# The second model's weights group by group instead of pair by pair, in a fused attention and expert kernel

## Chip, cores and metric

The kernel runs on one core of a Trainium2 chip. The metric is device time in microseconds, the median of three runs. The host only lays the inputs out; all arithmetic is on the core.

## The reference, cut to what matters

```python
kv = einsum('bhsd,bhse->bhde', k, v);  o = einsum('bhsd,bhde->bhse', q, kv)
x = (o / rms(o) * g_norm) as (2304, 512)
h = x @ w_in;  x = (h * sigmoid(h)) @ w_out          # first model, 2048 hidden units
p = domain_probs / (domain_probs.sum(-1) + 1e-9)
for e in range(4):                                   # second model, 1024 hidden units each
    out += p[:, e:e+1] * (maximum(x @ w1[e], 0) @ w2[e])
```

## The kernel before

The 2304 tokens are worked in three **pairs** of 768 tokens, each two halves of 384. The hidden units are cut into **groups** of 512: four groups of the first model, eight of the second (two for each expert). One **step** is one group for one pair: a first product (512 features to 512 hidden units), the activation, and a second product (512 hidden units to 512 outputs) that is added to `acc` in SBUF. Steps -12 to -1 belong to the first model, 0 to 23 to the second.

Every float32 operand of a product is split into a high part (rounded, by ScalarE, `hi`) and a low part (the rest, by VectorE or GpSimd, `lo`), and a product of blocks takes three matmul terms. A block product (`product`, L382 to 390) is 12 matmuls of 384 columns. A first product is always done with seven block products instead of eight (`first`, table `A`, `B`, `INTO`): that wants sums of weight blocks (`sumw`: s1 to s4) and sums of feature blocks (`xsum`: t1 to t4). A second product is done either plainly (`second`, eight block products, tile `ps_o`, 96 matmuls) or with seven (`again`, tiles `ps_ox` and `ps_oz`, 84 matmuls), which wants four sums of hidden blocks (`sumh`), three more hidden splits, and seven additions to `acc` (`gather`) instead of four. `seven(n)` says which steps use seven: before, steps 8 to 23, and five steps of the first model.

The order of the work is written out as events with slots (`events`, `seven_events`, `first_events`): a list of (slot, function), sorted, and emitted once. One slot is one block product on TensorE. `start[n]` is the slot at which step n begins; in a stretch of 14 or 15 slots TensorE alternates the seven first products of step n (slots 1, 3, 5, ...) with the second products of step n-1 (slots 0, 2, 4, ...). Each engine takes its instructions in that order, and so does SyncE's DMA queue (SP).

In the second model the **pair is the outer loop** (`pair(n) = n // 8`). The three pairs would each need all weights, so steps 0 to 7 make the split weights of a group (four loads of raw weights for each of the two matrices, eight sums, fourteen splits) and `put_away` writes them to `w_dram`; steps 8 to 23 `get` fourteen tiles of 512 KB each from there. The split features of a pair stay in SBUF for eight steps (`x_p`, seven tiles), and are made anew at steps 0, 8 and 16. Steps 0 to 7 have plain second products. When a pair is done, `leave` transposes it (L556), in later steps, and ScalarE's queue writes it out; the last pair leaves through `leave_last`.

```python
def seven(self, n): return n >= E2 or n in (-8, -7, -5, -4, -3)
def pair(self, n):  return (n + F1) % NP if n < 0 else n // E2
self.start[n + 1] = self.start[n] + (self.LONG if n <= E2 else self.SHORT)   # 15 or 14
```

Of the kernel before, what the change touches and what calls it, by code (L numbers as in the profile page):

```python
# [8 lines left out]
F32 = mybir.dt.float32  # L9
# [11 lines left out]
DM = H * D  # L21
# [44 lines left out]
class Net:  # L66
# [6 lines left out]

    A = ("a11", "a12", "s2", "s1", "s3", "s4", "a22")
# [9 lines left out]
    LONG, SHORT = 15, 14  # L84
    LEAD = 8

    def __init__(self, tc, dram, const, w, wd, out):
# [3 lines left out]
        self.p_dram, self.w_dram, self.x_dram = dram  # L91
# [8 lines left out]
        self.x, self.w1, self.wf, self.w2, self.raw, self.s, self.h, self.f, self.t, self.ps, self.pb = (  # L100
            {} for _ in range(11)
        )
# [26 lines left out]
    def plain_again(self):  # L129
        self.stacks["seven"].close()  # L130
        self.pb_p = self.open("left", "pb", 2)
        self.o_p = self.open("left", "o2", 2)
        self.s3_p = self.open("left", "s3", 3)
        self.raw3_p = self.open("left", "raw3", 4)

    def swap(self):
        self.stacks["conv"].close()
        self.s_p = self.open("sums", "s", 3, side="right")
        self.raw_p = self.open("sums", "raw", 8, side="right")

    def change(self):
        self.stacks["sums"].close()
        self.t_p = self.open("right", "t", 5, side="right")
        self.h7_p = self.open("right", "hid7", 1, side="right")

    def close(self):
        for k in ("right", "left", "psum"):
# [11 lines left out]

    def key(self, n):  # L160
        return n if n < 0 else n // E2
# [122 lines left out]
    def load1(self, n, i, j):  # L284
        t = self.raw_p.tile([128, 2, 2, 128], F32, tag="raw", name="raw1")
        for c in range(2):
            src = self.w[4 * n + 2 * i + c, :, 0, 256 * j : 256 * j + 256]
            self.nc.sync.dma_start(out=t[:, c, :, :].rearrange("p k f -> p (k f)"), in_=src)
        self.raw[n, 1, f"a{i + 1}{j + 1}"] = t.rearrange("p c k f -> p (c k f)")

    def load2(self, n, i, j, sums=False):
        pool = self.raw3_p if sums else self.raw_p
        t = pool.tile([128, 2, 256], F32, tag=pool.name, name=pool.name)
        for c in range(2):
            self.nc.sync.dma_start(out=t[:, c, :], in_=self.w[4 * n + 2 * j + c, :, 1, 256 * i : 256 * i + 256])
        self.raw[n, 2 + sums, f"a{i + 1}{j + 1}"] = t.rearrange("p c f -> p (c f)")

    def load_p(self, t, e):
        b = self.pb_p.tile([128, PW], F32, tag="pb", name="pb")
        src = self.p_dram.rearrange("(e b) k -> e (b k)", e=4)[e, t * PW : t * PW + PW]  # L300
        self.nc.sync.dma_start(out=b, in_=src.partition_broadcast(128))
        self.pb[t, e] = b

    def sumw(self, n, i, name, eng=None):
        a, b, op = self.SUMS[name]
        pool = self.s_p if i == 1 else self.s3_p
        t = pool.tile([128, 512], F32, tag=pool.name, name=pool.name)
        (eng or self.nc.vector).tensor_tensor(t, self.raw[n, i, a], self.raw[n, i, b], op=op)  # L308
        self.raw[n, i, name] = t

    def op1(self, n, k, eng=None):
        t = self.w1_p.tile([128, 2, 512], F32R, tag="w1", name="w1")
        self.split(t, self.raw[n, 1, self.A[k]], eng)
        self.w1[n, k] = t

    def op2(self, n, name, eng=None):
        pool, tag = (self.w2_p, "w2") if name[0] == "a" else (self.w1_p, "w1")
        t = pool.tile([128, 2, 512], F32R, tag=tag, name="w2")
# [759 lines left out]
```

## Time and profile before

| | before |
|---|---|
| median of 3 runs (lowest to highest) | 1168.19 us (1168.1 to 1168.59) |
| the profiled execution's own time | 1168.03 us |
| its span, first to last instruction | 1166.2 us |
| granted TensorE clock | 1.00 of full speed |
| TensorE (PE) busy | 1153.6 us, 99% |
| VectorE (DVE) busy | 866.8 us, 74% |
| ScalarE (ACT), GpSimd (POOL) busy | 499.1 us, 315.5 us |
| moved by DMA | 309 MB, mean 265 GB/s |

The profile is of one execution. Its parts used below: the page's head; the groups of instructions by line (busy time, mean ns of one, and the idle time of the engine ahead of them); the timeline, which gives start and duration of merged instructions and, in brackets, how long the engine had been idle before and who released it; the windows, which give busy time by engine in a stretch; and the DMA issues. PE's matmuls overlap, so a matmul's duration there is not the pitch at which they follow.

### The profile page before, as it was taken

How to read it: one execution, taken by the hardware profiler on the slowest of the kernel's cores; microseconds unless marked ns; L12 is line 12 of the kernel's file. 1: busy time of each engine (PE TensorE's matmuls, PEld its weight loads, DVE VectorE, ACT ScalarE, POOL GpSimd, SP SyncE). 2: the span in 40 equal slices, each digit the busy share in tenths (PEclk: the TensorE clock that was granted, in tenths of full speed). 3: DMA queues.
4: the chain of work that ended last, by engine and by line, in shares of the span. 5: the costliest groups of instructions: out<-in, count | busy, mean ns of one | idle time of the engine just before them, and what ended most of it. 6: DMA issues, size and time to landing. Idle time of an engine off the chain costs nothing.

```text
span 1166.2 us, 17617 instructions
## 1 busy us (share of the span) xinstructions
PE 1153.6 (99%) x6769; PEld 1144.8 (98%) x6769; DVE 866.8 (74%) x1010; ACT 499.1 (43%) x720; POOL 315.5 (27%) x196
## 2 busy tenths in 40 slices
PE   9999999999999999999999999999999999999998
PEld 8999999999999999999999999999999999999997
DVE  3997566887887667777777866777888866666776
ACT  4895565455544445434344324333233333233222
POOL 4943311232221324222232312121114221111112
PEclk9999999999999999999999999999999999999999
DMA  9876877566556366987896869898988777878764
GB/s 369 345 270 228 331 256 261 200 212 245 198 189 227 137 203 227 325 296 279 303 324 260 287 222 360 319 330 312 332 312 285 244 258 255 275 258 283 252 199 126
DMA packets 101815, 309.00 MB, mean 265 GB/s; under 512 B 11420, under 2 KB 37988, under 8 KB 101220
## 3 DMA queue, kind: packets, MB, share of 16 engines
q1 hardware_dynamic: 99716, 304.69, 73.6%
q10 hardware_dynamic: 2016, 3.18, 0.7%
q8 instruction: 54, 0.88, 0.3%
q14 instruction: 29, 0.24, 0.1%
HBM read 227.84 MB, written 79.99 MB: 264 GB/s over the span
## 4 chain that ended last, share of the span: by engine, by line
PE 54%; DVE 6%; ACT 2%; issue 2%; DMA 0%; SPq 0%; DVEq 0%; ACTq 0%
PE ps_x L390 15%; PE ps_z L390 11%; PE ps_o L526 10%; PE ps_ox L390 10%; PE ps_oz L390 8%; DVE f L469 1%; ACT hid L164 1%; DVE acc L495 1%; DVE f L433 1%; DVE hid L167 1%; DVE t L477 1%; DVE w L167 1%; PE ps_t L556 0%; DVE s L308 0%; ACT x L164 0%
## 5 line engine op out<-in xcount | busy, mean ns | idle before, releaser
L390 PE MATMUL ps_x<-x,w 128*128 128x384 f32 x1584 | 297.0, 335 | 0.0
L390 PEld LDWEIGHTS ps_x<-x,w 128*128 128x128 f32 x1584 | 277.6, 188 | 0.0
L526 PE MATMUL ps_o<-hid,w 128*128 128x384 f32 x1440 | 268.3, 335 | 1.5 <-ACT hid L164 1.4
L526 PEld LDWEIGHTS ps_o<-hid,w 128*128 128x128 f32 x1440 | 251.2, 188 | 3.4 <-ACT hid L164 2.4
L164 ACT ACTIVATE hid<-f 128x768 fp32r<-128x768 f32 x143 | 120.1, 843 | 243.3 <-DVE f L469 217.5
L390 PE MATMUL ps_z<-x,w 128*128 128x384 f32 x1188 | 222.9, 335 | 0.6 <-DVE f L433 0.6
L390 PEld LDWEIGHTS ps_z<-x,w 128*128 128x128 f32 x1188 | 208.2, 188 | 0.9 <-DVE f L433 0.9
L390 PE MATMUL ps_ox<-hid,w 128*128 128x384 f32 x1008 | 190.2, 336 | 1.2 <-DVE acc L495 1.0
L390 PEld LDWEIGHTS ps_ox<-hid,w 128*128 128x128 f32 x1008 | 176.2, 188 | 2.1 <-ACT hid L164 0.9
L167 DVE TENSOR_TENSOR hid<-f,hid 128x768 fp32r<-128x768 f32 x116 | 124.3, 1072 | 60.6 <-ACT hid L164 59.4
L390 PE MATMUL ps_oz<-hid,w 128*128 128x384 f32 x756 | 142.1, 335 | 1.6 <-DVE acc L495 1.2
L390 PEld LDWEIGHTS ps_oz<-hid,w 128*128 128x128 f32 x756 | 131.9, 188 | 2.7 <-DVE acc L495 2.1
L167 POOL TENSOR_TENSOR hid<-t,hid 128x768 fp32r<-128x768 f32 x32 | 62.7, 1961 | 241.8 <-ACT hid L164 236.0
L167 POOL TENSOR_TENSOR hid<-f,hid 128x768 fp32r<-128x768 f32 x27 | 52.3, 1938 | 210.7 <-ACT hid L164 210.7
L167 POOL TENSOR_TENSOR w<-raw,w 128x512 fp32r<-128x512 f32 x41 | 60.9, 1491 | 178.3 <-ACT w L164 135.2
L164 ACT ACTIVATE hid<-t 128x768 fp32r<-128x768 f32 x64 | 53.9, 843 | 121.0 <-DVE t L477 121.0
L495 DVE TENSOR_TENSOR acc<-ps_ox,acc 128x768 f32<-128x768 f32 x77 | 73.2, 950 | 41.7 <-PE ps_ox L390 41.6
L222 POOL TENSOR_TENSOR full<-full,wd_raw 128x512 int32<-128x512 int32 x32 | 47.7, 1491 | 127.7 <-DVE full L216 93.1
L433 DVE TENSOR_TENSOR f<-ps_z,f 128x768 f32<-128x768 f32 x66 | 62.6, 949 | 20.2 <-PE ps_z L390 20.2
L164 ACT ACTIVATE w<-s 128x512 fp32r<-128x512 f32 x88 | 54.3, 623 | 49.6 <-DVE s L249 18.1
L469 DVE SCALAR_TENSOR_TENSOR f<-f,pb 128x768 f32<-128x768 f32 x72 | 72.5, 1006 | 3.3 <-DMA pb<-p_dram 1.2
L495 DVE TENSOR_TENSOR acc<-ps_oz,acc 128x768 f32<-128x768 f32 x61 | 58.1, 952 | 20.1 <-PE ps_oz L390 19.2
(83 smaller groups left out, 1154.0 us busy)
## 6 DMA issues: line engine op xcount, KB each, us to landing
w<-w_dram SPq DMA_DIRECT2D x224, 512.0 KB, 5.0
w_dram<-w SPq DMA_DIRECT2D x112, 512.0 KB, 4.2
x<-x_dram SPq DMA_DIRECT2D x63, 768.0 KB, 4.6
raw<-in_w SPq DMA_DIRECT2D x192, 128.0 KB, 3.8
wd_raw<-in_wd SPq DMA_DIRECT2D x32, 512.0 KB, 4.4
x_dram<-x SPq DMA_DIRECT2D x21, 768.0 KB, 6.0
kv_raw<-in_kv SPq DMA_DIRECT2D x18, 512.0 KB, 10.2
q_raw<-in_qt SPq DMA_DIRECT2D x4, 1152.0 KB, 11.4
```

Source lines behind the costliest of these rows:

```text
L164: self.nc.scalar.activation(t[:, 0], f, AF.Copy)
L167: (eng or self.nc.vector).tensor_tensor(t[:, 1], f, t[:, 0].bitcast(F32), op=ALU.subtract)
L222: self.nc.gpsimd.tensor_tensor(f, f, self.words(c, i, 0, I32), op=ALU.add)
L390: self.nc.tensor.matmul(p[:, f, :HN], w[0][:, a, c : c + 128], x[:, b, kp, :], start=self.FRESH[k] and a == b == kp == 0, stop=b == kp == ...
L433: self.nc.vector.tensor_tensor(t, self.of_ps(n, c), t, op=ALU.add)
L469: self.nc.vector.scalar_tensor_tensor(f, src, 0.0, self.probs(n, int(name[2]) - 1), op0=ALU.max, op1=ALU.mult)
L477: self.nc.vector.tensor_tensor(f, self.f[n, a], self.f[n, b], op=ALU.subtract)
L495: self.nc.vector.tensor_tensor(a, self.of_ps(n, k), a, op=ALU.add)
L526: self.nc.tensor.matmul(self.ps[n, b][:, e, :HN], w[:, u, c : c + 128], h[:, v, kp, :], start=self.count[key] == 1, stop=self.count[key] = ...
```

## The change

1. The second model is worked **group by group, three pairs each**: `pair(n) = (n + 12) % 3`, `group(n) = (n + 12) // 3`, as in the first model.
2. A group's weights are loaded, summed and split once and stay in SBUF for its three steps (`weight_events`, `whi`, `flo`); `w_dram`, `put_away` and `get` go: 112 writes and 224 reads of 512 KB.
3. The split features are made at steps 0, 1 and 2, written to `x_dram` (21 tiles of 768 KB more) and fetched from there in steps 3 to 23 (`xget`, 147 more).
4. `seven(n)` is true from step 2 on: steps 2 to 7 get seven-block second products in place of eight. The step's length follows: 15 slots for steps 0 to 2, 14 after.
5. Sums of hidden blocks are written into the tile of one of their operands (`sumh`), so the pool `t` goes; three pools (`o2`, `s3`, `raw3`) go too. The splits of c11, c21 and t4 are set later within a step; c22's low part is on GpSimd in every step.
6. All three pairs are done only at the end: six `leave` calls, each with one copy of 128 x 1024 and one 512 KB write on SP's queue, stand among the last step's second products.
7. In steps 0 to 2 the first addition to each block of `acc` is a copy by ScalarE (before, in steps 0, 8 and 16).

The diff, cut to its core:

```diff
-            self.start[n + 1] = self.start[n] + (self.LONG if n <= E2 else self.SHORT)
+            self.start[n + 1] = self.start[n] + 7 + (7 if self.seven(n - 1) else 8)
     def seven(self, n):
-        return n >= E2 or n in (-8, -7, -5, -4, -3)
+        return n >= 2 or n in (-8, -7, -5, -4, -3)
     def pair(self, n):
-        return (n + F1) % NP if n < 0 else n // E2
+        return (n + F1) % NP
-    def put_away(self, n, i, k):
-        t = self.w1[n, k] if i == 1 else self.w2[n, self.A[k]]
-        self.nc.sync.dma_start(out=self.w_dram[n * 14 + (i - 1) * 7 + k], in_=t.bitcast(F32).rearrange("p a b -> p (a b)"))
-    def get(self, n, i, k):
...
     def sumh(self, n, name):
-        if n < 0:
-            f = self.f[n, dict(t1="c12", t2="c22", t3="c11", t4="c21")[name]]
-        else:
-            f = self.t_p.tile([128, 2, HN], F32, tag="t", name="t")
+        f = self.f[n, dict(t1="c12", t2="c22", t3="c11", t4="c21")[name]]
...
+        on_pool = {name: self.nc.gpsimd for name in (("t3", "t4") if n < 0 else ("c22", "t3", "t4"))}
+        late = 0 <= n < self.steps - 1
+        c11, c21, t4 = (5.8, 4.7, 5.6) if late else (4.7, 3.3, 4.6)
...
+    W1_AT = dict(
+        load=(-23.2, -13), s1=(-11, -7.6), s2=(-10.9, -7.5), s4=(-4.9, -5.1), s3=(-6.9, -4.5),
+        op=((-13.2, -11.2, -9.2, -7.2, -5.2, -3.2, -1.2), (-7.9, -7.8, -6.8, -5.8, 0.5, 6, 6.8)),
+    )
+    W2_AT = dict(
+        load=(-8, -4), s1=(5.5, 7.2), s2=(5.6, 7.5), s4=(9.4, 9.4), s3=(11, 9.6),
...
+    def weight_events(self, put, e):
+        b0, i = self.start[(e - E1) * NP], min(e - E1, 1)
...
+        on_pool = (self.A if i == 0 else ("a12", "s3", "a22")), (("a11", "a21", "a22") if i == 0 else ())
...
+            if n < NP:
+                at, sums = self.X_AT[n]
...
+                    put(b0 + at[k] + 2.5, self.xput, n, name)
+            else:
+                for k in range(7):
+                    put(self.start[n - 1] + 2 * k + 2.6, self.xget, n, k)
...
+        for k, at in enumerate((-2.5, 1.3, 2.8, 4.3, 5.8, 7.3)):
+            where = (self.ps2, self.steps) if at < 0 else (self.ps1, k + 1)
+            put(end + at, self.leave, k // 3, k % 3 * 2, *where)
```

How the order moves, at three places. **TensorE, step 3 with the second products of step 2.** In the rows `ps_x`, `ps_z` are first products, the others second products, `w_` a weight tile. Before:

```order
L390 MATMUL ps_z<-x_3939,w_4657 128x384 x12
L526 MATMUL ps_o<-hid,w_4489 128x384 x6
L526 MATMUL ps_o<-hid,w_4578 128x384 x6
L390 MATMUL ps_x<-x_3973,w_4701 128x384 x12
```

And now:

```order
L366 MATMUL ps_ox<-hid,w_4115 128x384 x12
L366 MATMUL ps_x<-x_4545,w_4636 128x384 x12
L366 MATMUL ps_oz<-hid,w_4097 128x384 x12
L366 MATMUL ps_z<-x_4587,w_4639 128x384 x12
L366 MATMUL ps_ox<-hid,w_4784 128x384 x12
```

The plain second product (two halves of 6 matmuls on each slot, 16 halves in a step) has become seven whole block products between seven first products; one block product of 12 is gone from each of steps 2 to 7.

**VectorE, ahead of a new group** (`hid<-f,hid` a low part of a hidden block, `f<-f` a sum of hidden blocks, `acc<-ps` an addition to `acc`, `f<-ps_z,f` the c11 or c12 addition, `f<-f,pb` relu and probability, `s<-raw` and `w_<-` sums and low parts of weights). Before, in a step that fetches its weights:

```order
L167 TENSOR_TENSOR hid<-f,hid 128x768
L433 TENSOR_TENSOR f<-ps_z,f 128x768
L469 SCALAR_TENSOR_TENSOR f<-f,pb 128x768
L495 TENSOR_TENSOR acc<-ps_ox,acc 128x2x384
L167 TENSOR_TENSOR hid<-f,hid 128x768
L495 TENSOR_TENSOR acc<-ps_oz,acc 128x2x384
L495 TENSOR_TENSOR acc<-ps_ox,acc 128x2x384
L433 TENSOR_TENSOR f<-ps_x,f 128x768
```

And now, in the step before a new group:

```order
L149 TENSOR_TENSOR hid<-f,hid 128x768
L289 TENSOR_TENSOR s<-raw_5310,raw_5331 128x512
L289 TENSOR_TENSOR s<-s,raw_5334 128x512
L149 TENSOR_TENSOR w_5422<-raw_5334,w_5422 128x512
L464 TENSOR_TENSOR acc<-ps_oz,acc 128x2x384
L149 TENSOR_TENSOR w_5453<-s,w_5453 128x512
L149 TENSOR_TENSOR w_5470<-s,w_5470 128x512
L289 TENSOR_TENSOR s<-raw_5355,s 128x512
L464 TENSOR_TENSOR acc<-ps_ox,acc 128x2x384
L289 TENSOR_TENSOR s<-raw_5334,raw_5310 128x512
L411 TENSOR_TENSOR f<-ps_x,f 128x768
```

Between two additions to `acc` there now stand up to four sums and splits of the next group's weights. A second run of the same kind (s4, a11, s1, s2, then two more sums) stands 14 slots later.

**TensorE, the end.** Before:

```order
L390 MATMUL ps_x<-x_8825,w_10573 128x384 x12
L390 MATMUL ps_ox<-hid,w_10594 128x384 x12
L390 MATMUL ps_oz<-hid,w_10623 128x384 x12
L390 MATMUL ps_ox<-hid,w_10652 128x384 x12
L390 MATMUL ps_oz<-hid,w_10684 128x384 x12
```

And now:

```order
L366 MATMUL ps_x<-x_10012,w_9624 128x384 x12
L366 MATMUL ps_ox<-hid,w_9617 128x384 x12
L522 MATMUL ps_t<-ident,acc 128x128 x8
L366 MATMUL ps_oz<-hid,w_9645 128x384 x12
L522 MATMUL ps_t<-ident,acc 128x128 x8
L366 MATMUL ps_ox<-hid,w_9662 128x384 x12
L522 MATMUL ps_t<-ident,acc 128x128 x16
L366 MATMUL ps_oz<-hid,w_9786 128x384 x12
```

The 48 transposes of the first two pairs have moved from the middle of the program to between the last second products (8 of them just ahead of the last first product).

## Rows read from the trace of the kernel before

**Rows 1.** The page's head: span, busy time, and the clock in 40 slices

```profile
span 1166.2 us, 17617 instructions
...
PE 1153.6 (99%) x6769; PEld 1144.8 (98%) x6769; DVE 866.8 (74%) x1010; ACT 499.1 (43%) x720; POOL 315.5 (27%) x196
...
PEclk9999999999999999999999999999999999999999
```

**Rows 2.** Groups of instructions by line: the plain second products

```profile
L526 PE MATMUL ps_o<-hid,w 128*128 128x384 f32 x1440 | 268.3, 335 | 1.5 <-ACT hid L164 1.4
```

**Rows 3.** Timeline of PE in steps 1 and 2: first and last of 24 block products

```profile
424.14 2.25 PE L390 MATMUL ps_x<-x,w 128*128 128x384 f32 x12
...
474.21 4.33 PE L526 MATMUL ps_o<-hid,w 128*128 128x384 f32 x24
```

**Rows 4.** Timeline of PE, 150 to 1150 us: every row with idle time ahead

```profile
247.79 2.32 PE L390 MATMUL ps_ox<-hid,w 128*128 128x384 f32 x12 [0.61 <-DVE acc L495]
253.21 2.38 PE L390 MATMUL ps_oz<-hid,w 128*128 128x384 f32 x12 [1.01 <-DVE acc L495]
297.70 2.35 PE L390 MATMUL ps_oz<-hid,w 128*128 128x384 f32 x12 [0.38 <-ACT hid L164]
...
414.70 0.96 PE L526 MATMUL ps_o<-hid,w 128*128 128x384 f32 x4 [0.59 <-ACT hid L164]
...
570.76 2.68 PE L526 MATMUL ps_o<-hid,w 128*128 128x384 f32 x12 [0.38 <-ACT hid L164]
...
665.68 2.68 PE L526 MATMUL ps_o<-hid,w 128*128 128x384 f32 x12 [0.44 <-ACT hid L164]
...
920.07 2.36 PE L390 MATMUL ps_z<-x,w 128*128 128x384 f32 x12 [0.60 <-DVE f L433]
922.80 2.35 PE L390 MATMUL ps_ox<-hid,w 128*128 128x384 f32 x12 [0.37 <-DVE acc L495]
...
1147.26 2.35 PE L390 MATMUL ps_ox<-hid,w 128*128 128x384 f32 x12 [0.19 <-issue]
1149.82 2.35 PE L390 MATMUL ps_oz<-hid,w 128*128 128x384 f32 x12 [0.20 <-DVE acc L495]
```

**Rows 5.** Windows: busy PE, PEld, DVE, ACT, POOL (instructions), clock, DMA share, GB/s

```profile
880.00:940.00 60.00, 59.03 (x338) 58.39 (x337) 53.23 (x54) 22.08 (x29) 19.87 (x9) 1.00 0.74 255
...
1000.00:1060.00 60.00, 60.00 (x353) 59.93 (x352) 40.93 (x45) 18.45 (x24) 11.12 (x6) 1.00 0.79 268
```

**Rows 6.** Groups by line on DVE and POOL: sums and low parts of weights

```profile
L167 DVE TENSOR_TENSOR w<-s,w 128x512 fp32r<-128x512 f32 x74 | 56.8, 769 | 19.4 <-ACT w L164 19.4
...
L308 DVE TENSOR_TENSOR s<-raw,raw 128x512 f32<-128x512 f32 x32 | 32.0, 1000 | 0.0
...
L167 POOL TENSOR_TENSOR w<-raw,w 128x512 fp32r<-128x512 f32 x41 | 60.9, 1491 | 178.3 <-ACT w L164 135.2 <-DMA raw<-in_w 31.5 <-issue 11.6
```

**Rows 7.** Timeline of a step late in the second model: VectorE's last relu, then TensorE

```profile
1116.10 0.95 DVE L469 SCALAR_TENSOR_TENSOR f<-ps_x,pb 128x768 f32<-128x768 f32 x1
...
1119.77 2.25 PE L390 MATMUL ps_z<-x,w 128*128 128x384 f32 x12
```

**Rows 8.** Timeline at step 16: a POOL and a DVE instruction that overlap

```profile
915.60 1.87 POOL L167 TENSOR_TENSOR x<-acc,x 128x768 fp32r<-128x768 f32 x1
915.91 2.37 DVE L167 TENSOR_TENSOR hid<-f,hid 128x768 fp32r<-128x768 f32 x1 [1.42 <-ACT hid L164]
```

**Rows 9.** DMA issues: count, KB each, median us to landing

```profile
x<-x_dram SPq DMA_DIRECT2D x63, 768.0 KB, 4.6
...
out<-o SPq DMA_DIRECT2D x3, 384.0 KB, 2.6
```

**Rows 10.** Timeline: transposes of a finished pair, and the program's last copy

```profile
751.68 1.03 PE L556 MATMUL ps_t<-ident,acc 128*128 128x128 f32 x8
...
1161.96 0.49 ACT L571 ACTIVATE o<-ps_t 128x384 f32<-128x384 f32 x1 [0.30 <-ACT o L571]
```

**Rows 11.** The page: GB/s in 40 slices

```profile
GB/s 369 345 270 228 331 256 261 200 212 245 198 189 227 137 203 227 325 296 279 303 324 260 287 222 360 319 330 312 332 312 285 244 258 255 275 258 283 252 199 126
```

More of the change, by code (lines that the diff above doesn't have):

```diff
@@ L301, in load_p, with sumw @@
         self.nc.sync.dma_start(out=b, in_=src.partition_broadcast(128))
-        self.pb[t, e] = b
-    def sumw(self, n, i, name, eng=None):
+        self.pb[n] = b
+    def sumw(self, e, i, name):
         a, b, op = self.SUMS[name]
[L306 to L314, printed above, removed]
@@ new lines, in whi, with done_raw @@
+    def whi(self, e, i, name):
+        pool, tag = (self.w1_p, "w1") if i == 1 else (self.v_p, "w2b") if name in ("s3", "s4") else (self.w2_p, "w2")
+        t = pool.tile([128, 2, 512], F32R, tag=tag, name=f"w{i}")
+        self.halves[e, i, name] = t, self.raw[e, i, name]
+        self.hi(*self.halves[e, i, name])
+        if i == 1:
+            self.wf[e, self.A.index(name)] = t
+        else:
+            self.w2["f", e, name] = t
+    def done_raw(self, e, i, *names):
+        for name in names:
+            del self.raw[e, i, name]
@@ L690, in seven_events, with plain_events @@
         for m, g in enumerate(self.GATHER):
-            put(after + 2 * m + (1.1 if m < 6 else 0.25), self.gather, n, *g)
+            for d in (0, 1) if n == self.steps - 1 and m == 6 else (None,):
+                put(after + 2 * m + (1.1 if m < 6 else 0.25 if n < 0 else 0.45), self.gather, n, *g, d)
         put(after + 11.2, self.ps.pop, (n, "oz"))
-        put(after + 12.26, self.ps.pop, (n, "ox"))
+        put(after + 12.46, self.ps.pop, (n, "ox"))
+    def plain_events(self, put, n):
+        after, blocks = self.start[n + 1], self.blocks(n)
+        for b, (i, j) in enumerate(blocks):
+            for d in range(2):
+                put(after + 4 * b + 2 * d, self.second, n, b, d)
+            put(after + 4 * b + 3.2, self.gather, n, b, i, j)
+            put(after + 4 * b + 3.21, self.ps.pop, (n, b))
+        for i in range(2):
+            for j in range(2):
+                end = [4 * max(b for b in range(4) if blocks[b][m] == (i, j)[m]) + 2.1 for m in range(2)]
+                for m in range(2):
+                    put(after + end[1], self.h.pop, (n, f"b{m + 1}{j + 1}")) if i == 0 else None
+                    name = f"a{i + 1}{m + 1}"
+                    if j == 0 and n == self.last_use(n, name):
+                        put(after + end[0], self.w2.pop, ("f", self.group(n), name))
@@ new lines, in events @@
+            for k in range(7):
+                put(b0 + 1 + 2 * k, self.first, n, k)
+            for slot, f, c, name in (
+                (2.1, self.keep, "x", "c11"), (4.1, self.add, "z", "c11"), (6.1, self.keep, "x", "c12"),
+                (8.1, self.keep, "z", "c22"), (10.1, self.add, "x", "c22"), (12.1, self.add, "z", "c12"),
+            ):
+                put(b0 + slot, f, n, c, name)
+            put(b0 + 12.2, self.ps.pop, (n, "z"))
+            for slot, name in ((4.3, "c11"), (10.3, "c22"), (12.25, "c12"), (14.05 if n else 13.1, "c21")):
+                put(b0 + slot, self.relu, n, name)
@@ new lines, in events @@
+            put(b0 + 14.06, self.ps.pop, (n, "x"))
+            put(b0 - 8, self.load_p, n)
+            put(b0 + 14.07, self.pb.pop, n)
+            if self.seven(n):
+                self.seven_events(put, n)
+            else:
+                for slot, name in ((5.3 if n else 6.15, "c11"), (10.5, "c22"), (12.5, "c12"), (14.1, "c21")):
+                    put(b0 + slot, self.hhi, n, name)
+                    put(b0 + slot + 0.01, self.hlo, n, name, pool if name == "c22" else None)
+                self.plain_events(put, n)
```

321 lines of the change are left out of this document (92 added, 229 removed), and 3 rows, old and new, of the table X_AT.

## Prediction

> **What bounds the kernel now.** I read the page's head first. PE is busy for 99% of the span, every other engine for 74% or less, and the clock row is 9 in all 40 slices, so the clock neither costs nor gives anything [rows 1]. Then the timeline of PE: block products of 12 matmuls follow each other at a fixed pitch. From 424.14 to 474.21 us there are 24 of them, (474.21 - 424.14) / 24 = 2.0863 us each [rows 3]. A "slot" of the order is therefore 2.0863 us, a stretch of 14 slots 29.21 us, one of 15 slots 31.29 us. Then every place from 150 to 1150 us at which PE idled [rows 4]: ten rows, 4.77 us together, and only those after 414 us can be touched by the change. So the time is the number of block products times their pitch, plus a few stalls. What can take the gain back is an engine that comes so late that PE has to wait, and the windows say which: VectorE is busy for 53.23 of 60 us around step 16 (89%), and for 40.93 of 60 us in steps that only fetch weights (68%) [rows 5].
>
> **The change, part by part.** The sum is made against the profiled execution's own 1168.03 us, which lies 0.16 us under the median of 1168.19.
>
> Block products. The plain second products are 1440 matmuls [rows 2], 15 steps of 96; six of these steps become seven-block ones of 84. The order of the changed kernel shows one block product fewer in each of steps 2 to 7 and otherwise the same ones: 6 x 2.0863 = **-12.52 us**, all of it on the engine that sets the end.
>
> Stalls that go with them. At 570.76 and 665.68 PE waited for ScalarE's split of a hidden block ahead of a plain second product [rows 4], those of steps 4 and 7, which are no longer plain: 0.38 + 0.44 = **-0.82 us**. The wait at 414.70 is of the same kind, but five steps of 31.29 us ahead of 570.76, in the first model's last step, which stays. So do the three rows before 300 us.
>
> The change of pair. In steps 1 and 2 VectorE makes the next pair's feature sums and low parts. Before, this stood at steps 8 and 16: at step 16 it cost 0.60 + 0.37 = 0.97 us, at step 8 there is no row [rows 4]. These go, and the same work comes back at steps 1 and 2, where the first additions to `acc` are on ScalarE, but some of the third group's weights stand beside it. Bounds: 0 and 2 x 0.97 = 1.94. I take what the two changes cost before, 0.97: **-0.97 + 0.97**.
>
> The change of group, the open term. Seven times a new group's eight sums and eleven low parts stand on VectorE between the work of hidden blocks. At 1.000 us for a sum of raw blocks (taken for all) and 0.769 for a low part [rows 6] that is 8 x 1.000 + 11 x 0.769 = 16.5 us per group. A step without weights takes 40.93 / 60 x 29.21 = 19.9 us of VectorE [rows 5], so a group of three steps 59.8 + 16.5 = 76.3 of 87.6 us, 87%: about as full as the 89% window that cost 0.97 us. It isn't spread evenly: seven of these pieces stand in slots -7.6 to -4.5 and eight in 6.4 to 9.6, between the two places of a step where VectorE is fullest. What is queued behind them are the c22 addition, the relus and the hidden sums; the relu of c21 must be over before PE's second first-product of the next step overwrites its bank. In a step without weights that relu ended at 1116.10 + 0.95 = 1117.05 and the product began at 1119.77 [rows 7], so VectorE may come 2.72 us later than now before PE waits. Bounds: 0 if the slack takes it, and 7 x 0.97 = 6.79 if each change of group costs what the fullest step cost. Nearest in kind are steps 1 to 7 of before, each of which made a whole group's fourteen splits in one step and which together show 0.82 us of stalls [rows 4]. I take **+0.82**.
>
> VectorE's other additions (four hidden sums and three additions to `acc` in each of six steps, 42 instructions) lie in those 87%. ScalarE's three more splits in each lie beside a row that shows it at 18.45 of 60 us [rows 5].
>
> The port between VectorE and GpSimd. At 915.91 a VectorE subtract took 2.37 us, where GpSimd had begun one at 915.60 that ended at 917.47: VectorE's ended 0.81 us after that [rows 8]. It looks as if it stood still until GpSimd was through. Three GpSimd subtracts of 1.491 us [rows 6] per group, 4.47 us, are beside VectorE's clusters, so they can add to its lateness; the slack of 2.72 us takes about two of them if the cluster itself fits. The Trainium skill, "SBUF — State Buffer", section "SBUF: two separate sides", says that GpSimd and a VectorE instruction with two SBUF inputs hold the shared ports exclusively, the other blocking for the whole instruction. By that rule the two clusters would lose up to 4.47 us per group; by the row alone one overlap is shown; the trace agrees with the rule there. My sum goes by the slack, and the rule's way is the first rival.
>
> Weights and features by DMA. 336 transfers of 512 KB go, 168 of 768 KB come, -176 + 132 MB. A fetched feature tile is asked for 12.4 slots = 25.9 us ahead of its product and such a transfer lands in 4.6 us [rows 9]; it waits first for the product that frees the tile, which ends 0.6 slots before. Cost nothing; if that cover of 21 us were gone, the first product of each step would wait. The raw weights stand on the same queue behind at most one waiting fetch (two slots, 4.2 us) and are asked for 5.4 slots = 11.3 us ahead of their sums.
>
> The end. The 48 transposes stay the same (eight take 1.03 us in either place [rows 10]), but now stand between the last second products, where PE waited 0.19 + 0.20 us for VectorE [rows 4]: **-0.39**. Six more writes of 512 KB are on the queue of the last five. If the last write stood behind three of them, 1.57 MB at the highest rate shown, 369 GB/s [rows 11], is 4.3 us; the last write of before needs 2.6 us [rows 9] after a copy at 1161.96 [rows 10]. The sixth is issued some five products (10 us) earlier, so I take 0; bounds 0 and +4.3.
>
> Sum: 1168.03 - 12.52 - 0.82 - 0.97 + 0.97 + 0.82 - 0.39 = **1155.1 us**.
>
> **Rivals.**
>
> Slower: GpSimd holds up VectorE at each change of group, beyond the slack. The place: the low parts of a12 (slot -7.4) and a22 (slot 7.2) on GpSimd, beside VectorE's sums. The price if both reach PE in full: 2 x 1.491 = 2.98 us, seven times 20.9, on a sum without new stalls of 1168.03 - 12.52 - 0.82 - 0.97 - 0.39 = 1153.3: 1174.2 us. It decides from (1168.03 - 1153.3) / 7 = 2.1 us per group on. For it: the overlap at 915.91, and 87% load. Against it: VectorE's additions from PSUM stand in the same stretches, and the 2.72 us of slack must be used up first. Chance 0.06.
>
> Each change of group costs as step 16 did: 1153.3 + 0.97 + 6.79 = 1161.1 us. For it: 87% against 89%. Against it: step 16 had feature work of 128x768 that nothing spread. Chance 0.15.
>
> No new stall anywhere: 1153.3 us. For it: the slack. Chance 0.15.
>
> The six writes reach the end: 1155.1 + 4.3 = 1159.4 us. Chance 0.06.
>
> The change doesn't remove the block products: excluded by the order, but a stall in features or weights that I do not see would come here, 0.03.
>
> **How the numbers follow.** The forecast's own case (a few tenths per group at most, 1154 to 1157) has 0.55. With the case of no stall below and that of 0.97 per group above, the range is 1153.0 to 1161.2; left out are the slower rival, the unseen stall and some of the tails. A measurement of this kernel tells about 0.2% from no change, 2.3 us: faster means under 1165.9. Every case but the slower rival and part of the unseen one lies under that: faster 0.92, same 0.02, slower 0.06.
>
> **What would show it.** In the changed profile: 72 matmuls fewer in all, `ps_o` at 864; pitch 2.086 us again; clock row all 9. Right: PE's timeline has rows with idle time of under 0.3 us at each change of group (every 87.6 us from step 3 on), VectorE's busy time near 80%, in windows of a whole group 85 to 90%. The slower rival would show as PE waiting for VectorE's `f` or `acc` twice per group, with VectorE subtracts of 2 us and more beside a GpSimd one. The case of the writes would show in the stretch between the last copy and the end, above 4 us. I would be wrong if `x` tiles from `x_dram` or raw weights release PE, ScalarE or VectorE anywhere, or if waits in steps 0 to 2 come to over 2 us.

## The result, and the profile after

| | before | after |
|---|---|---|
| median of four runs each | 1168.22 us | 1150.13 us (1149.51 to 1150.42) |
| the profiled execution's own time | 1168.03 us | 1150.29 us |
| its span | 1166.2 us | 1148.5 us |

The ratio is 0.9844, with a 95% interval from 0.9827 to 0.9861. The forecast was 1155.1 us with a range from 1153.0 to 1161.2: the sign is right, the gain was too small by 5 us, and the time lies under the range. The table and the sums below compare the profiled executions, 17.74 us apart; the medians are 18.1 us apart.

The head of the page after, beside [rows 1]:

```profile
span 1148.5 us, 17121 instructions
...
PE 1138.0 (99%) x6697; PEld 1132.7 (99%) x6697; DVE 926.5 (81%) x1065; ACT 512.1 (45%) x725; POOL 324.8 (28%) x194
...
PEclk9999999999999999999999999999999999999999
```

72 matmuls fewer, the clock at the same level in all slices, VectorE at 81% where "near 80%" was written. The groups of instructions by line show the plain second products, beside [rows 2], at 864 in place of 1440, 576 fewer; the seven-block ones have 504 more (`ps_ox` and `ps_oz` together 2268 in place of 1764), which makes the 72. The idle time of PE ahead of the plain ones is now 0:

```profile
L495 PE MATMUL ps_o<-hid,w 128*128 128x384 f32 x864 | 159.8, 335 | 0.0
```

The pitch of the block products, beside [rows 3], from the timeline of PE across a change of group. 24 block products lie between the start of the first row and that of the last: (645.04 - 594.96) / 24 = 2.0867 us.

```profile
594.96 2.25 PE L366 MATMUL ps_ox<-hid,w 128*128 128x384 f32 x12
...
645.04 1.21 PE L366 MATMUL ps_oz<-hid,w 128*128 128x384 f32 x6
```

The rows of PE with idle time ahead, beside [rows 4], are down to three in the first model and one among the last transposes. Between 300 and 1143 us there is none:

```profile
248.79 2.32 PE L366 MATMUL ps_ox<-hid,w 128*128 128x384 f32 x12 [0.61 <-DVE acc L464]
254.21 2.38 PE L366 MATMUL ps_oz<-hid,w 128*128 128x384 f32 x12 [1.00 <-DVE acc L464]
298.60 2.32 PE L366 MATMUL ps_oz<-hid,w 128*128 128x384 f32 x12 [0.28 <-ACT hid L146]
```

VectorE is as full as was worked out (87%). The windows, with the columns of [rows 5], show an emptier step, a fuller one, and eight steps together, 204.05 of 234 us:

```profile
506.00:535.00 29.00, 29.00 (x169) 29.00 (x168) 22.79 (x26) 14.06 (x20) 8.53 (x5) 1.00 0.69 241
564.00:594.00 30.00, 30.00 (x174) 30.00 (x174) 26.94 (x30) 10.35 (x14) 7.76 (x4) 1.00 0.80 271
506.00:740.00 234.00, 234.00 (x1348) 234.00 (x1347) 204.05 (x222) 88.86 (x123) 60.05 (x32) 1.00 0.66 226
```

So the load came as forecast and no wait of PE followed from it. The transfers and the end, beside [rows 9] and [rows 10], from the DMA issues and the timeline of ScalarE: from the start of the last copy 1148.5 - 1144.41 = 4.1 us are left, where before 1166.2 - 1161.96 = 4.2 were. The six writes don't reach the end.

```profile
x<-x_dram SPq DMA_DIRECT2D x210, 768.0 KB, 4.3
...
out<-o SPq DMA_DIRECT2D x6, 512.0 KB, 2.8
```

```profile
1144.41 0.49 ACT L536 ACTIVATE o<-ps_t 128x384 f32<-128x384 f32 x1 [0.31 <-ACT o L536]
```

**How much a wait really was.** The idle time in brackets was taken for the price of a stall. Here is the neighbourhood of the stall at 570.76 of the kernel before, from the timeline of PE; the row between these two stands in [rows 4]:

```profile
568.13 2.25 PE L526 MATMUL ps_o<-hid,w 128*128 128x384 f32 x12
...
573.28 1.03 PE L390 MATMUL ps_x<-x,w 128*128 128x384 f32 x5
```

From 568.13 to 570.76 are 2.63 us, from there to 573.28 another 2.52; two products at their pitch take 4.17. So this stall cost 0.98 us, while the bracket says 0.38. The bracket begins where the modelled end of the last matmul lies (a matmul is shown as 0.335 us long, though they follow at 0.174), and the matmul that starts after a wait is followed some 0.1 us later than the pitch, too. A second wait inside the same product, at 571.75, is 0.03 us of idle time and costs 0.30. Counted like this, from the starts of single matmuls, the stalls of before that are gone are: 0.95 (570), 1.00 (665), 1.51 (919 and 922), 0.90 (1147 and 1149), and 0.86 + 0.26 (414 and 422), 5.48 us in all.

| term, us | forecast | measured |
|---|---|---|
| six block products | -12.52 | -12.52 |
| stalls at 570 and 665 | -0.82 | -1.95 |
| stalls at 919 and 922 | -0.97 | -1.51 |
| the same work at steps 1 and 2 | +0.97 | 0 |
| seven changes of group | +0.82 | 0 |
| waits of the last second products | -0.39 | -0.90 |
| stalls at 414 and 422 | 0 | -1.12 |
| beginning, up to the first product of the first model | 0 | +1.01 |
| not traced | 0 | -0.75 |
| sum | -12.91 | -17.74 |

The beginning is not of the change: that first product starts at 140.45 us before and 141.46 after, and in two variants of the kernel before below at 140.54 and 141.36.

### The profile page after: what moved, and what is told of

It is laid out like the page before. It is cut to its first block, busy times and chain, and to the rows that moved or that the text cites. A ratio compares the mean times of both kernels' runs of the same rounds, so it can differ in the third digit from the quotient of the medians.

```text
span 1148.5 us, 17121 instructions
## 1 busy us (share of the span) xinstructions
PE 1138.0 (99%) x6697; PEld 1132.7 (99%) x6697; DVE 926.5 (81%) x1065; ACT 512.1 (45%) x725; POOL 324.8 (28%) x194
## 4 chain that ended last, share of the span: by engine, by line
PE 90%; DVE 4%; DMA 3%; ACT 2%; issue 0%; POOL 0%; SPq 0%; ACTq 0%; POOLq 0%; DVEq 0%
PE ps_x L366 22%; PE ps_ox L366 19%; PE ps_z L366 17%; PE ps_oz L366 14%; PE ps_o L495 12%; PE ps_h L394 4%; DMA kv_raw<-in_kv 2%; DVE hid L149 1%; PE p_o L855 1%; DMA wd_raw<-in_wd 1%; ACT hid L146 1%; PE ps_kv L833 1%; DVE acc L464 1%; DVE w L149 1%; PE p_t L882 0%; DVE f L451 0%
## 5 line engine op out<-in xcount | busy, mean ns | idle before, releaser
L146 ACT ACTIVATE hid<-f 128x768 fp32r<-128x768 f32 x225 | 187.3, 843 | 369.4 <-DVE f L451 188.1
L149 POOL TENSOR_TENSOR hid<-f,hid 128x768 fp32r<-128x768 f32 x78 | 154.0, 1975 | 534.3 <-ACT hid L146 414.9
L366 PE MATMUL ps_ox<-hid,w 128*128 128x384 f32 x1296 | 243.3, 335 | 0.6 <-DVE acc L464 0.6
L366 PEld LDWEIGHTS ps_ox<-hid,w 128*128 128x128 f32 x1296 | 226.4, 188 | 0.9 <-ACT hid L146 0.9
L149 DVE TENSOR_TENSOR hid<-f,hid 128x768 fp32r<-128x768 f32 x147 | 150.3, 1024 | 54.1 <-ACT hid L146 53.8
L366 PE MATMUL ps_oz<-hid,w 128*128 128x384 f32 x972 | 182.7, 336 | 1.3 <-DVE acc L464 1.0
L495 PE MATMUL ps_o<-hid,w 128*128 128x384 f32 x864 | 159.8, 335 | 0.0
L495 PEld LDWEIGHTS ps_o<-hid,w 128*128 128x128 f32 x864 | 150.9, 188 | 0.0
L451 DVE TENSOR_TENSOR f<-f 128x768 f32<-128x768 f32 x108 | 107.2, 992 | 3.2 <-ACT f L421 1.8
L406 ACT ACTIVATE f<-ps_x 128x768 f32<-128x768 f32 x66 | 53.3, 807 | 42.4 <-PE ps_x L366 42.3
L149 DVE TENSOR_TENSOR w<-s,w 128x512 fp32r<-128x512 f32 x74 | 52.2, 713 | 6.3 <-ACT w L146 5.7
```

Of the source, the lines that this page charges most:

```text
L146: self.nc.scalar.activation(t[:, 0], f, AF.Copy)
L149: (eng or self.nc.vector).tensor_tensor(t[:, 1], f, t[:, 0].bitcast(F32), op=ALU.subtract)
L366: self.nc.tensor.matmul(p[:, f, :HN], w[0][:, a, c : c + 128], x[:, b, kp, :], start=self.FRESH[k] and a == b == kp == 0, stop=b == kp == ...
L406: self.nc.scalar.activation(t, self.of_ps(n, c), AF.Copy)
L451: self.nc.vector.tensor_tensor(f, self.f[n, a], self.f[n, b], op=ALU.subtract)
L495: self.nc.tensor.matmul(self.ps[n, b][:, e, :HN], w[:, u, c : c + 128], h[:, v, kp, :], start=self.count[key] == 1, stop=self.count[key] = ...
```

## Experiments

The theory after the result: the time is block products times a fixed pitch, nothing new makes PE wait, and the error is stalls that were priced too low or added without need. The rival: something else became faster, or new waits are there and are paid for by a gain not seen. A time is the median of its runs, beside the kernel before on the same chip.

**1. Plain second products in steps 2 to 5 again** (the sums of second weights of those two groups, needed no longer, are left out).

```diff
-        return n >= 2 or n in (-8, -7, -5, -4, -3)
+        return n >= 6 or n in (-8, -7, -5, -4, -3)
```

> The changed kernel with plain second products again in steps 2 to 5 (their groups need no sums of second weights then). Theory A, the time is block products times 2.086 us plus PE's waits, and the new order has no waits of its own: 4 more block products, 1150.1 + 4 x 2.086 = 1158.5 us, no idle row of PE between 300 us and the end. Rival B, plain second products bring back their own waits for ScalarE's split, 0.95 us start to start as at 570 us before: 1158.5 + 4 x 0.95 = 1162.3 us.

1158.76 us (before 1168.59; ratio 0.9918, 0.9904 to 0.9933). Against the changed kernel +8.6, and four block products are 4 x 2.087 = 8.35. No wait of PE between 300 us and the last transposes. The price of a block product stands.

**2. The kernel before with another order inside the plain second product**, in all steps and not only up to step 0: in the first block of outputs the terms with high parts of hidden blocks go ahead of those with low parts, the earlier hidden block first.

```diff
-        if b == 0 and NP - F1 <= n <= 0:
+        if b == 0 and NP - F1 <= n:
```

> The kernel before with one line of the change alone: a plain second product's first block begins with the matmuls on the hidden blocks that are ready first, in all plain steps (before, only up to step 0). Theory A, this order is what kept PE waiting at 570 and 665 us (start to start 0.95 and 1.00 us beyond the pitch): those rows go, 1168.2 - 1.95 = 1166.3 us. Rival B, the split is late because VectorE is overfull in those steps, and PE waits a few matmuls later instead: 1168.2 us, the rows only move.

1166.92 us against 1168.59 (ratio 0.9987, 0.9977 to 0.9996): -1.7. The stalls at 570 and 665 are gone from the trace, the others are where they were. This measures the two stalls by themselves: 1.7 us, near the 1.95 counted from starts and twice the 0.82 that the brackets give. The same line is part of the change, though the list of the change doesn't name it; it is in force in experiment 1, whose plain steps show no such wait.

**3. The two tiles that hold two of the feature blocks, exchanged as before.** This item wasn't seen in the change: `slot` (L328 to 330) chooses which of two SBUF tiles takes which of the feature blocks 2 and 3. Before, the exchange holds at pairs 0 and 2, after only at step 1 and in the first model.

```diff
-        return 5 - k if k in (2, 3) and (n < 0 or n == 1) else k
+        return 5 - k if k in (2, 3) and n != 1 else k
```

> The changed kernel with the feature tiles of t1 and t2 exchanged as they were before (exchanged in steps 0 and 2 on, not in step 1). Theory A, the two waits at 413.8 and 421.6 us of before (0.86 and 0.26 us start to start) came from ScalarE standing at the split of t1, whose tile was freed 4 us later: they return, 1150.1 + 1.1 = 1151.2 us. Rival B, they went because the writes of split weights left the queue: 1150.1 us.

1151.56 us (1151.33 to 1151.72), +1.4 against the changed kernel, and the two stalls are back. From the timeline of PE of this run:

```profile
415.47 0.96 PE L495 MATMUL ps_o<-hid,w 128*128 128x384 f32 x4 [0.59 <-ACT hid L146]
```

Why they came: in the kernel before, ScalarE's split of a feature block at 398.16 waited for a product that was still reading the tile, and what was queued behind it, splits of hidden blocks among them, was late. The first row is ScalarE's timeline before, the second the same split after, which waits for nothing:

```profile
398.16 0.85 ACT L164 ACTIVATE x<-acc 128x768 fp32r<-128x768 f32 x1 [2.70 <-PE ps_z L390]
```

```profile
396.24 0.83 ACT L146 ACTIVATE x<-acc 128x768 fp32r<-128x768 f32 x1
```

**4. Seven-block second products from step 0 on**, to see whether two more block products can go (weights and feature work of steps 1 and 2 set earlier to fit).

```diff
-        return n >= 2 or n in (-8, -7, -5, -4, -3)
+        return n >= 0 or n in (-8, -7, -5, -4, -3)
```

> The changed kernel with seven-block second products from step 0 on. Theory A, VectorE's slack takes the extra hidden sums and additions also where the features of the next pair are made: two block products fewer, 1150.1 - 2 x 2.086 = 1145.9 us. Rival B, steps 0 to 2 have no slack left: PE waits 1 to 1.5 us in each of two steps, 1148 to 1149 us.

1149.98 us (1149.81 to 1150.09): two block products fewer, -4.17, and no gain that can be told. PE waits in steps 1 and 2:

```profile
465.67 2.38 PE L366 MATMUL ps_oz<-hid,w 128*128 128x384 f32 x12 [0.25 <-DVE acc L464]
470.93 2.35 PE L366 MATMUL ps_ox<-hid,w 128*128 128x384 f32 x12 [0.79 <-DVE acc L464]
497.23 2.35 PE L366 MATMUL ps_oz<-hid,w 128*128 128x384 f32 x12 [1.00 <-DVE acc L464]
502.04 2.38 PE L366 MATMUL ps_ox<-hid,w 128*128 128x384 f32 x12 [0.37 <-DVE acc L464]
```

From start to start these and a smaller one at 510.68 come to 3.75 us, more than either theory gave. Here is what the forecast had feared, VectorE too late with its additions; it begins where feature work and seven-block additions fall together, two steps earlier than the change goes.

**5. VectorE delayed, to measure its slack**: two reductions of 128x512 more, at slot 12.2 of the first step of each of seven groups; then six.

```diff
+    spin = const.tile([128, 8], F32, name="spin"), blank
...
+        for _ in range(2):
+            self.nc.vector.reduce_sum(self.spin[0][:, :4], self.spin[1].unsqueeze(1).to_broadcast([128, 4, 128]), axis=AX.X)
...
+            if e > E1:
+                put(self.start[(e - E1) * NP] + 12.2, self.delay)
```

> The changed kernel with two idle reductions of 128x512 (about 0.69 us each, one SBUF input) on VectorE at slot 12.2 of the first step of each of seven groups. In the changed kernel's trace the relu of c21 in that step ends 1.60 us before TensorE begins to overwrite its bank, in the next step 2.75, in the third 2.03. Theory A, that margin is all that stands between VectorE's lateness and PE: 1.4 us fit, 1150.1 us. Rival B, another deadline is nearer (a hidden split, an addition to acc): PE waits in each group, up to 7 x 1.4 = 9.8 us more, 1160.

> The same with six reductions, about 4.1 us, in the same place. Theory A: 4.1 - 1.6 = 2.5 us reach PE in each of seven groups, and some 0.15 for the restart, 18.6 us: 1168.7. Rival B, VectorE catches up only partly, or a nearer deadline decides: 7 x 4.1 = 28.7 us, 1179.

1159.49 us with two (before 1168.61; ratio 0.9922, 0.9904 to 0.9939) and 1171.29 with six (ratio 1.0024, 1.0015 to 1.0034). With two the time is that of the second theory, but its cause isn't there: after 300 us PE waits nowhere. What is longer is each matmul, see 8. With six, PE waits once per group, 1.94 us beyond the pitch in six groups and 0.59 in the first. VectorE's timeline and then PE's:

```profile
626.51 4.28 DVE L707 TENSOR_REDUCE spin<-blank 128x4 f32<-128x512 f32 x6
...
634.44 0.95 DVE L465 TENSOR_TENSOR acc<-ps_ox,acc 128x768 f32<-128x768 f32 x1
```

```profile
635.54 2.32 PE L367 MATMUL ps_oz<-hid,w 128*128 128x384 f32 x12 [1.70 <-DVE acc L465]
```

Together these are 12.2 us, where the medians of the two runs are 11.8 apart. A delay of 1.4 us is hidden, one of 4.28 is hidden but for 1.94. The deadline that is met first is an addition to `acc`, which frees the PSUM tile of the next `ps_oz` product, not the relu of c21 that the forecast took. In the changed kernel the same two pairs, from its timeline:

```profile
626.15 0.95 DVE L464 TENSOR_TENSOR acc<-ps_ox,acc 128x768 f32<-128x768 f32 x1
...
627.88 0.95 DVE L446 SCALAR_TENSOR_TENSOR f<-ps_x,pb 128x768 f32<-128x768 f32 x1
...
628.34 2.25 PE L366 MATMUL ps_oz<-hid,w 128*128 128x384 f32 x12
...
630.43 0.86 PE L366 MATMUL ps_z<-x,w 128*128 128x384 f32 x4
```

The addition ends at 627.10, 1.24 us ahead of its product; the relu ends at 628.83, 1.60 ahead of its own. The forecast's 2.72 us was of a step without weights. More than 1.24 us can be hidden because VectorE wins some back: the relu ahead of this chain takes 1.85 us in the changed kernel (at 621.52), beside a GpSimd low part that began at 620.71, and 0.95 in both runs with reductions, where it comes after that one has ended.

**6. The later places of c11, c21 and t4 undone**, the item that the forecast didn't price; then c11 alone, and c21 with t4. The early places are those that the first model's steps have. In the second model of the kernel before only c21's 3.3 was the same: c11 was split at 5.3, and t4 summed at 1.16 and split at 5.5.

```diff
-        late = 0 <= n < self.steps - 1
+        late = False
```

> The changed kernel with the old places of c11's, c21's and t4's splits within a step (4.7, 3.3, 4.6 instead of 5.8, 4.7, 5.6). Theory A, the steps have 1.6 us or more to spare and no single place matters: 1150.1 us, no idle row. Rival B, those later places are what keeps PE from waiting: idle rows in steps 2 to 22, 0.3 to 1 us in each group, 1152 to 1157 us.

> The changed kernel with the split of c11 alone back at slot 4.7 (the change has 5.8); c21 and t4 stay late. With all three early the time was 1179.3 us, and each change of group showed two waits of TensorE: one of 1.86 to 1.90 us from start to start ahead of a second product for an addition to acc, and one of 2.61 us in the next step for a low part of a weight. Theory A (the places of c21 and t4 carry it): 1150.1 us, no wait after 300 us. Theory B (c11's split, queued in order ahead of the relu and the additions, carries it): 1170 to 1179 us. If each carries one of the two waits: some 12 to 17 us of loss here, 1162 to 1167.

> The counterpart: c11 late as in the change, c21's split (slot 3.3, its low part straight behind it) and the sum t4 (4.6) early as before. Theory A (c21 and t4 carry it): 1170 to 1179 us, with both waits per group. Theory B (c11 carries it): 1150.1 us. If each carries one of the two waits: 1162 to 1167.

All three early: 1179.32 us (ratio 1.0093, 1.0077 to 1.0109), 29 us more than the changed kernel. c11 alone: 1150.10, nothing. c21 and t4: 1168.17 us (ratio 1.0001, 0.9991 to 1.001), 18 us more. So c21 and t4 carry the larger part, and c11, which does nothing alone, adds 11 us when they are early. With all three early the changed kernel is slower than the one before, and with c21 and t4 early it is as slow. There PE waits twice in each of six groups, both times ahead of a `ps_oz` product: 0.82 us beyond the pitch (0.48 in the first group) and 2.00, together 16.6 us. All three early, timeline of PE in one group:

```profile
631.73 2.32 PE L366 MATMUL ps_oz<-hid,w 128*128 128x384 f32 x12 [1.52 <-DVE acc L464]
...
646.93 3.61 PE L366 MATMUL ps_ox<-hid,w 128*128 128x384 f32 x11 [2.27 <-DVE w L149]
```

The second wait costs 2.5 us in each of the other groups and 3.97 in this one, because here the granted clock fell to the lower of its two levels, 1.2 GHz, while PE stood for these 2.27 us; until about 650.1 the matmuls that follow are 0.32 us apart. The windows of this run, with the columns of [rows 5]:

```profile
647.00:650.00 3.00, 3.00 (x10) 3.00 (x11) 1.95 (x3) 0.00 (x0) 0.00 (x0) 0.50 0.31 129
```

How it comes, from GpSimd's and VectorE's timelines of the run with c21 and t4 early:

```profile
610.93 1.85 POOL L149 TENSOR_TENSOR hid<-f,hid 128x768 fp32r<-128x768 f32 x1 [4.56 <-ACT hid L146]
...
611.61 1.98 DVE L149 TENSOR_TENSOR hid<-f,hid 128x768 fp32r<-128x768 f32 x1 [0.84 <-ACT hid L146]
...
630.30 0.95 DVE L464 TENSOR_TENSOR acc<-ps_ox,acc 128x768 f32<-128x768 f32 x1
```

VectorE comes to a low part before ScalarE has made the high one, waits 0.84 us with everything else queued behind it, and the chain up to the addition that frees `ps_oz` ends at 631.25, where PE's product was due at 629.47: the wait of 1.76 us in brackets. In the changed kernel the addition `f<-ps_x,f` ahead of that chain starts 2.2 us ahead of the `ps_ox` product beside it (617.81 and 620.00), here 0.8 us behind it (621.96 and 621.12): VectorE is 3.0 us later, more than the 1.24 us of slack.

The wait for ScalarE is only part of that. The low part at 611.61 also runs beside one of GpSimd's and takes 1.98 us, and so does the one ahead of it (at 605.14: a wait of 0.78 us, then 2.03). In the changed kernel the same two low parts, c21's at 606.47 and c11's at 608.32, stand clear of GpSimd's, wait for nothing and take 0.95 us each; the second of them:

```profile
608.32 0.95 DVE L149 TENSOR_TENSOR hid<-f,hid 128x768 fp32r<-128x768 f32 x1
```

So the early places add 1.6 us of waiting and 2.1 us of longer low parts, against which other instructions of the stretch gain something. No run separates the two.

**7. GpSimd's low part that ran beside the stall at 919, put on VectorE, in the kernel before.**

```diff
-pool if k in (1, 3, 5) and t == 0 or k in (0, 1, 5) and t else None
+pool if k in (1, 3, 5) and t == 0 or k in ((0, 1, 5) if t == 1 else (0, 1)) and t else None
```

> The kernel before with the low part of b22 of the third pair (step 16) on VectorE instead of GpSimd, the instruction beside which VectorE's split of c21 took 2.37 us. Theory A, the waits at 919.1 and 922.1 us (0.76 and 0.54 us beyond the pitch) come from VectorE standing still at the shared port: 1.4 us less of standing against 0.9 us of work more, the waits shrink to under half, total 0.5 to 1 us less. Rival B, VectorE is simply overfull there: the waits grow by up to 0.9 us.

One run, 1169.26 us, where the kernel before has a median of 1168.61 and reaches 1169.26: no answer by the time. By the trace the waits around 919 and 922 come to 1.43 us in place of 1.51, in three pieces; the low part on VectorE takes 1.28 us itself. The run exchanges 1.42 us of standing (2.37 us against 0.95) for 1.28 us of work, so that nearly equal waits fit either theory: whether GpSimd's hold on VectorE caused that stall stays open.

**8. Where in SBUF the operands lie.** The runs with reductions had a tile of 32 bytes per partition more. Repeated with 64 bytes, and then without any reduction, an unused tile of 32, 96, 128 and 224 bytes, and 96 in the kernel before.

```diff
+    pad = const.tile([128, 8], F32, name="pad")
+    nc.gpsimd.memset(pad, 0.0)
```

> The changed kernel with the same two reductions of 128x512 at every change of group as in the run with two reductions, but the small constant tile they write to is 64 bytes per partition long in place of 32, so that everything placed behind it in SBUF starts a further 32 bytes on. In that earlier run TensorE never waited for VectorE after 300 us, yet its matmuls followed each other at a mean of 175.5 ns in every stretch of the span, where the changed kernel has 173.9; 6000 x 1.6 ns = 9.6 us is the whole loss. Theory A (the 32 byte tile moved the operands, the reductions themselves are hidden): the pitch is 173.9 again and the time 1150.1 us, within 0.5. Theory B (the reductions on VectorE slow TensorE, or any shift does): the pitch stays at 175.5 and the time at 1159.5.

> The changed kernel with nothing but one unused constant tile of 32 bytes per partition more, written once at the start; no instruction of VectorE is added. Theory A (a shift of the operands by 32 bytes lengthens every matmul's pitch): pitch 175.5 ns in all stretches and 1159.5 us. Theory B (the pitch in the earlier run came from the reductions): pitch 173.9 and 1150.1 us.

> The changed kernel with one unused constant tile of 96 bytes per partition. The runs with 32 and 64 bytes cost 9 to 10 us, with every block product of 12 matmuls at a mean pitch of 175.5 ns instead of 173.9, also first products, whose own operands had not moved. In the changed kernel the operands of the second products (hidden blocks and second weights) begin at multiples of 128 bytes and those of the first products (features, first weights) 96 bytes past one; 96 bytes more bring both to the same place. Theory A (what counts is that the two kinds, which alternate on TensorE, lie at different places with the second at a multiple of 128): pitch 175.5 and 1159.2 us again. Theory B (what counts is the distance between the two kinds, and equal places are best): pitch 173.9 or lower, and 1150.1 us or less; at the 173.4 ns that the later matmuls of a product show it would be 1147.

> The changed kernel with one unused constant tile of 128 bytes per partition, so that all places are those of the changed kernel again, modulo 128 bytes. Theory A (the place modulo 128 bytes sets the pitch): pitch 173.9 and 1150.1 us, within 0.5. Theory B (any further tile, or the instruction that writes it, costs the 1.6 ns): pitch 175.5 and 1159.2 us.

> The changed kernel with an unused tile of 224 bytes, which is 96 + 128. Shifts by 32, 64 and 128 bytes cost 9 us, 96 gained 3. Modulo 128 bytes all operands of the long matmuls now stand at 96, as with 96 bytes; modulo 256 or 512 they don't stand alike (the hidden blocks and second weights are 128 bytes away from the features and first weights). Theory A (the place modulo 128 bytes): 173.3 ns and 1147.3 us. Theory B (the place modulo a larger number, 256 or 512 bytes; that a shift by 128 bytes was slow where no shift at all was not, speaks for it): 175.5 ns and 1159 us.

> The kernel before with the same unused tile of 96 bytes per partition. With it the changed kernel's matmuls followed each other at 173.3 ns in every stretch, without the slower first matmuls of each block product that it shows without the tile (173.9 ns on the mean), and the time fell from 1150.1 to 1147.3 us. In the kernel before the two kinds of operands stand 96 bytes apart too, as in the changed one. Theory A (both kernels stood at the same pitch of 173.9 ns, so the placement has no share in the difference between them): pitch 173.3, time 1168.2 - 6589 x 0.00055 = 1164.6 us, and the difference between the kernels with the tile is the 18 us of before. Theory B (the change had moved the operands to a better or worse place): the kernel before gains much less or more than 3.6 us here.

| kernel | tile, bytes | mean pitch of the matmuls, ns | median, us |
|---|---|---|---|
| changed | none | 173.9 | 1150.13 |
| changed, two reductions per group | 64 | 175.5 | 1159.81 |
| changed | 32 | 175.5 | 1159.16 |
| changed | 96 | 173.3 | 1147.26 (ratio 0.9816, 0.9801 to 0.9831) |
| changed | 128 | 175.5 | 1158.82 |
| changed | 224 | 173.6 | 1148.34 (ratio 0.9828, 0.9812 to 0.9845) |
| before | none | 173.9 | 1168.56 |
| before | 96 | 173.4 | 1166.05 (ratio 0.9979, 0.9969 to 0.9988) |

The timelines of PE, 24 block products each, with 32 bytes and with 96: (644.69 - 594.13) / 24 = 2.1067 us and (643.68 - 593.76) / 24 = 2.0800.

```profile
594.13 2.27 PE L366 MATMUL ps_ox<-hid,w 128*128 128x384 f32 x12
...
644.69 2.27 PE L366 MATMUL ps_ox<-hid,w 128*128 128x384 f32 x12
```

```profile
593.76 2.24 PE L366 MATMUL ps_ox<-hid,w 128*128 128x384 f32 x12
...
643.68 2.24 PE L366 MATMUL ps_oz<-hid,w 128*128 128x384 f32 x12
```

The reductions cost nothing, the tile costs 9 us: with it and no reduction the time is the same. It moves the operands of the second products (hidden blocks, second weights), while features and first weights stay; yet the products of both kinds become slower, in every stretch of the span. Inside a block product with 32, 64 or 128 bytes the matmuls from the third to the seventh after a change of product are the long ones, up to 185 ns, and the last five take 173.3; with 96 bytes all twelve take 173.3. In the changed kernel as it is, the hidden blocks and second weights begin at multiples of 128 bytes, features and first weights 96 past one; 96 and 224 bytes bring all of them to 96, and these are the two fastest. The place modulo 128 can't be all of it, since 128 bytes more restore the changed kernel's places and give the slow pitch. One count puts all six placements in order, the distance between the two kinds of places modulo 256 bytes, taken the shorter way: 0 gives 173.3 ns, 128 gives 173.6, 96 (the changed kernel) 173.9, 64 and 32 give 175.5. Modulo 512 it is the same here. No run was made to test it, and why it should be so stays open.

For the question of this change it is settled: both kernels stood at 173.9 ns, and the tile of 96 bytes helps both (2.5 us before, where 3.6 were expected, and 2.9 after). With the tile in both they are 18.8 us apart, without it 18.1, so the placement doesn't make the gain. The version with the tile of 96 bytes is the fastest here: 1147.26 us, 2.9 us under the changed kernel and 21 under the kernel before.

## Why the prediction was right and wrong

**Right.** The block products: 6 at the pitch of before, 12.52 us, and experiment 1 gives the same price the other way. The load of VectorE, 87%. The transfers: no row after 300 us shows PE waiting for a feature tile or a weight. The end: six writes hidden, and the transposes fill the waits of the last second products.

**Wrong: "I take +0.82" for the seven changes of group, and "-0.97 + 0.97" for the change of pair.** Neither shows a wait, together 1.79 us too much. The case of no new stall had its chance of 0.15, and is what came. The reason named for it, "the slack takes it", holds, though by another deadline: the addition ahead of `ps_oz`, with 1.24 us left, and not the relu with 2.72. That it holds is due to the places of c21 and t4, an item of the change that had no term; without it the time is 18 to 29 us longer (experiment 6). The estimate by load was no measure of either outcome: the same instructions at 87% cost 0 or 29 us by their order.

**Wrong: the sizes of the stalls that go.** The step "0.38 + 0.44 = -0.82" measured 1.95 by starts and 1.7 by experiment 2; "0.60 + 0.37 = 0.97" measured 1.51, and "-0.39" 0.90. The mechanism was right each time, though the stalls at 570 and 665 would have gone by the other order of experiment 2 alone, and the bracket was the wrong reading, 2.18 us in all.

**Wrong: "The wait at 414.70 is of the same kind, but ... in the first model's last step, which stays."** It goes, with the one at 422, 1.12 us: the change exchanges two tiles, and experiment 3 puts the stalls back by that alone.

These come to 1.79 + 2.18 + 1.12 = 5.09; the beginning took 1.01 and 0.75 isn't traced, which makes the 4.8 us. With no new stall and stalls by starts, and with 414 left in place, the sum would have been 1168.03 - 12.52 - 4.36 = 1151.2.

**The slower rival** fell: the hold is there, but in the changed kernel it didn't reach PE. In the changed kernel's timeline a GpSimd and a VectorE instruction overlap again, as in [rows 8]:

```profile
639.45 2.16 POOL L149 TENSOR_TENSOR hid<-f,hid 128x768 fp32r<-128x768 f32 x1 [4.55 <-PE ps_oz L366]
...
639.83 2.33 DVE L149 TENSOR_TENSOR w<-raw,w 128x512 fp32r<-128x512 f32 x1
```

GpSimd ends at 641.61 and VectorE at 642.16, 0.55 later, where such an instruction takes 0.68 in other rows. The Trainium skill, "SBUF — State Buffer", section "SBUF: two separate sides", says the one that comes second is blocked for the whole instruction of the other; the trace agrees here with 2.33 against 0.68 us. It says nothing of whether that time reaches the end; the slack decided that here. With the early places of experiment 6 the same hold is part of the 3.0 us by which VectorE came too late, so the rival's mechanism was real and its chance of 0.06 hung on an item that the forecast hadn't weighed.

## What to carry to other kernels

Price a stall by the distance from start to start against the pitch around it, not by the idle time in the brackets; here that doubled it. When an engine is nearly full, look for its nearest deadline among all that it releases, and at the order of its instructions there: the average load told nothing of whether the change would cost 0 or 29 us. In an experiment that adds a tile, compare the pitch of the matmuls first, or run the tile alone, before the time is put down to what was added.

## What was not expected of the hardware

The pitch of identical matmuls depends on where operands lie in SBUF: 173.3, 173.6, 173.9 or 175.5 ns for 384 columns, with shifts of 32 to 224 bytes between the operands of alternating products, at the same granted clock. The products whose own operands had not moved are slowed as well. A loss of 9 us in a span of 1150 appeared with a tile that nobody reads.

A wait of PE costs more than its gap: after it, the first matmul is followed at about 0.25 to 0.28 us in place of 0.174, some 0.1 us on each wait of the traces here.

One wait of 2.27 us, in the run with all three splits early, went with a granted clock of 0.50 for a little over 3 us; five waits of 2.24 to 2.27 us in the same run did not.
